# Dealing the inversion's row steps to the slots by their size

## The chip, the cores and the metric

The kernel runs on one core of one Trainium2 chip. The metric is the device time of one execution in microseconds. The times of the kernel before are 2229.79, 2228.49 and 2227.1 us, so the median is 2228.49 us. One further execution was profiled; it took 2232.75 us, of which 2230.4 us lie between its first and its last instruction. The engines are called PE (TensorE), DVE (VectorE), ACT (ScalarE), POOL (GpSimd) and SP (the engine that issues most DMAs).

## What is computed

The reference is a chain of three parts. A delta-rule attention goes through 768 tokens, a soft mixture of eight experts follows, and an MLP closes it:

```
for t in range(768):                     # attention, state 48x48 per head
    y[t] = q[t] @ state
    state = state + b[t] * outer(k[t], v[t] - k[t] @ state)
P = exp(x @ w_gate - max)                # 3072 tokens, 8 experts
for _ in range(8):                       # Sinkhorn
    P /= P.sum(1) + 1e-9;  P /= P.sum(0) + 1e-9;  P *= 3072 / 8
x2 = sum over e of P[:, e] * (relu(x @ w1[e]) @ w2[e])
h = x2 @ w_in;  out = (h * sigmoid(1.702 * h)) @ w_out
```

## The kernel before

The attention is worked in 24 units `u` of 64 tokens for two batches at once, six groups `g` of four units. For a group, the triangular systems inside its units must be inverted first. This is `prep(g)` (line 209), a generator. It computes Gram blocks on PE (tile `pg`, line 182) into `am`, transposes them on DVE into `ln` (line 269), and then inverts 32x32 blocks by rows in a loop over `jj` from 1 to 30. Each `jj` has two DVE instructions: a product into `lt` (line 279) and an addition into `ln` (line 283), both over (31-jj)*jj elements in each of 128 partitions. So they are small at both ends of the loop, 30 elements, and largest in its middle, 240. After the loop DVE transposes the result to `ta` (line 314) and `tt` (line 340), and PE joins the 32x32 blocks to 64x64 (`pz`, line 323, and `px`, line 332). In this text "loop g" is the loop over `jj` of group g; loops 1 to 5 run while the units of the group before are worked.

A unit itself is `chain(u)` (line 357), a serial recurrence in four steps: PE multiplies keys with the state `S` (`ks`, line 373) and DVE makes `r` of it (line 375); PE solves with the inverse (`up`, line 384); PE forms the update (`sp`, line 395) and DVE the new `S` (line 401); PE forms the output (`y`, line 408). One unit later PE transposes the output (`xt`, line 421), ACT and DVE split it into a high and a low part (`xb`, by `split`, lines 495 and 496).

Beside this PE has the first expert as filler: `expert0` (line 642) is cut into 480 items of three matmuls each (`ph` or `po`, lines 499 to 501). ACT and DVE take the `ph` results on (`h`, lines 653 and 654).

The order in which the instructions are written is the order in each engine's queue. It is dealt out by `slot(t)` (line 743), called after each of the 96 steps of the chain. It draws pieces from `prep` until the sum of what they yielded reaches the slot's number in `PIECES` (`FIRST` for the first 16 slots); an item of `prep` yields 1.0, and each half of a `jj` yields 0.5. Between the pieces it calls `expert`, which writes as many items as are due; the share that is due before a piece is weighted with the size of the piece before it. What is left of the 480 items is written after the attention, five at a time between the steps of the Sinkhorn iteration (`psk`, line 711). Then the other experts and the MLP follow, to the end.

Of the kernel before, what the change touches and what calls it, by code (L numbers as in the profile page):

```python
# [40 lines left out]
class Attention:  # L41
# [167 lines left out]
    def prep(self, g):  # L209
# [65 lines left out]
        for jj in range(1, 31):  # L275
            tmp = self.one.tile([128, 256], F32, tag="lt", name="lt")
            nr = 31 - jj
            t3 = tmp[:, 0:nr * jj].rearrange("p (a c) -> p a c", c=jj)
            nc.vector.tensor_tensor(  # L279
                out=t3, in0=ln[:, jj + 1:32, jj:jj + 1].to_broadcast([128, nr, jj]),  # L280
                in1=ln[:, jj:jj + 1, 0:jj].to_broadcast([128, nr, jj]), op=ALU.mult)
            yield 0.5
            nc.vector.tensor_tensor(out=ln[:, jj + 1:32, 0:jj], in0=ln[:, jj + 1:32, 0:jj], in1=t3, op=ALU.add)  # L283
            if (g, jj) in self.at:
                self.at[g, jj]()
            if 0 < g < NG - 1:
                if jj == 17:
                    self.square(w + 2)
                elif jj == 21:
                    self.norm(w + 2)  # L290

            if jj == 22 and 0 < g < NG - 1:
                step = self.weights(w + 2)
            elif jj > 22 and 0 < g < NG - 1:
                next(step, None)
            if jj == 30 and 1 < g < NG - 1:
                self.mask(u + 4)
                self.mask(u + 5)
            yield 0.5
        if g < 2:  # L300
            nc.gpsimd.tensor_copy(out=self.gate, in_=ln[:, 31, 29:30])
            if g == 0:
# [158 lines left out]
def kernel(  # L461
# [257 lines left out]
    def expert_item():  # L719
        while ex:  # L720
            if next(ex[0], None) is not None:
                return True
            ex.pop(0)
        return False
# [5 lines left out]
    while A.ready < 0:  # L730
        next(prep)
# [4 lines left out]
    def expert(n):  # L736

        nonlocal done, due
        due += n
        while done < due and expert_item():  # L740
            done += 1

    def slot(t):

        n, k = rate * ITEMS[t % 16] if t >= LAG else 0, (PIECES if t > 15 else FIRST)[t % 16]
        if t == LAG:
            expert(BURST)
        i = 0
        while i < k:
            expert(n / (k + 1) * step[0])  # L750
            step[0] = next(prep, 1.0)
            i += step[0]
        expert(n / (k + 1))

    step = [1.0]
    build = sums(0, 0)
    for u in range(NU):
        for s, _ in enumerate(A.chain(u)):
            if s == 1 and u > 0:
                if 4 * u >= LAG:  # L760
                    due -= 1
                    expert(1)
                    done += expert_item()
                while u % 2 == 1 and len(ex) > 1:
                    done += expert_item()
                emit_x(u - 1, A.xt())
                if u % 2 == 0:
                    ex.append(expert0(u // 2 - 1))
            if s > 1 and u > 0 and u % 2 == 0:
                (logits if s == 2 else turn)(u // 2 - 1)  # L770
            slot(4 * u + s)
            while A.ready < u // 4:
                next(prep)
            if u > 12:
                next(build, None)
        if u % 2 == 1 and u // 2 + 4 < 12:
            A.load_k(u // 2 + 4)
            A.load_x(u // 2 + 4)
# [415 lines left out]
```

## Time and profile before

| stretch of the profiled execution | us | PE busy | DVE busy | granted PE clock |
|---|---|---|---|---|
| start, first inversion | 0 to 45 | 24.13 | 32.51 | 0.89 |
| first units | 45 to 77 | 23.15 | 23.81 | 0.50 |
| loop 1 | 77 to 115 | 27.30 | 34.14 | 0.74 |
| between loops 1 and 2 | 115 to 165 | 47.84 | 22.18 | 0.83 |
| loop 2 | 165 to 195 | 28.03 | 28.52 | 1.00 |
| between loops 2 and 3 | 195 to 240 | 45.00 | 22.18 | 0.96 |
| loop 3 | 240 to 270 | 28.32 | 28.59 | 1.00 |
| between loops 3 and 4 | 270 to 314 | 43.97 | 23.64 | 1.00 |
| loop 4 | 314 to 344 | 26.41 | 28.45 | 0.94 |
| between loops 4 and 5 | 344 to 390 | 45.43 | 24.26 | 1.00 |
| loop 5 | 390 to 419 | 26.25 | 27.45 | 1.00 |
| last units | 419 to 499 | 80.00 | 19.41 | 0.96 |
| Sinkhorn | 499 to 540 | 34.01 | 29.48 | 0.83 |
| experts and MLP | 540 to 2230 | 1676.98 | 1182.14 | 1.00 |

The profiled execution took 2232.75 us and its span is 2230.4 us. The clock is a share of full speed: 1.00 is 2.4 GHz, 0.50 is 1.2 GHz, and a value between says how long each held. A busy PE may be a slow one, so both columns are read together. DVE instructions have a few tens of ns between them that do not count as busy, so 28.5 of 30 us is an engine without a pause.

### The profile page before, as it was taken

What the parts mean: (1) busy time and instruction counts of PE and PEld (TensorE: products, weight loads), DVE (VectorE), ACT (ScalarE), POOL (GpSimd) and SP (SyncE); (2) the same over time, 40 slices, a digit from 0 to 9 for tenths busy, and PEclk for the clock granted to TensorE, in tenths of its full rate; (3) what the DMA queues carried; (4) which work ended last, traced back from release to release, by engine and by line L of the source; (5) the groups of instructions that cost most, each with busy time, mean ns of one, the idle gap of its engine ahead of it and who ended that gap; (6) DMA issues with size and microseconds to landing.
All of it is one profiled execution on the core that took longest, in us unless ns stands there. A gap on an engine that the chain in (4) does not pass through costs nothing.

```text
span 2230.4 us, 40903 instructions
## 1 busy us (share of the span) xinstructions
PE 2156.8 (97%) x15663; PEld 1953.7 (88%) x15663; DVE 1526.7 (68%) x2792; ACT 1068.0 (48%) x2126; POOL 1096.8 (49%) x1275
## 2 busy tenths in 40 slices
PE   5799999998999999999999999999999999999999
PEld 4778888896989999999999999999999989889998
DVE  7847775627777777767776777777775556776676
ACT  4334434434444544444445444455544446565554
POOL 4141123224776776666552656556665434662333
PEclk8689999998999999999999999999999999999999
DMA  6223333348335343333448655565554465567231
GB/s 159 51 62 81 105 100 102 90 127 294 136 115 184 124 168 136 115 144 110 159 164 275 185 178 182 170 200 178 188 199 143 136 239 164 172 192 246 92 121 50
DMA packets 229154, 336.74 MB, mean 151 GB/s; under 512 B 15648, under 2 KB 192416, under 8 KB 224800
## 3 DMA queue, kind: packets, MB, share of 16 engines
q1 hardware_dynamic: 228096, 332.86, 46.1%
q8 instruction: 123, 2.02, 0.4%
q10 hardware_dynamic: 864, 1.28, 0.2%
q14 instruction: 71, 0.58, 0.1%
HBM read 204.58 MB, written 129.50 MB: 150 GB/s over the span
## 4 chain that ended last, share of the span: by engine, by line
PE 85%; DVE 9%; DMA 2%; POOL 1%; ACT 1%; issue 1%; SPq 0%; POOLq 0%; ACTq 0%; DVEq 0%
PE po L501 14%; PE po L499 14%; PE po L500 14%; PE c L500 11%; PE c L501 11%; PE c L499 11%; DVE lt L279 3%; DVE ln L283 3%; PE ph L499 1%; PE pg L182 1%; PE ph L500 1%; PE ph L501 1%; PE y L408 1%; PE sp L395 1%; PE px L332 1%
## 5 line engine op out<-in xcount | busy, mean ns | idle before, releaser
L501 PE MATMUL po<-w2c,h 128*128 128x384 f32 x1728 | 586.6, 339 | 1.4 <-DVE h L1007 1.3
L500 PE MATMUL po<-w2c,h 128*128 128x384 f32 x1728 | 587.3, 340 | 0.0
L499 PE MATMUL po<-w2c,h 128*128 128x384 f32 x1728 | 578.5, 335 | 1.1 <-ACT h L1005 1.1
L1062 POOL TENSOR_TENSOR acc<-acc,ye 128x384 f32<-128x384 f32 x252 | 261.6, 1038 | 381.7 <-ACT ye L1061 329.6
L501 PE MATMUL c<-xt,w1c 128*128 128x512 f32 x1080 | 429.1, 397 | 2.0 <-POOL w1c L496 2.0
L499 PE MATMUL c<-xt,w1c 128*128 128x512 f32 x1080 | 424.5, 393 | 4.4 <-DVE f L1039 2.3
L500 PE MATMUL c<-xt,w1c 128*128 128x512 f32 x1080 | 428.0, 396 | 0.0
L1039 DVE TENSOR_TENSOR o<-o,c 128x512 f32<-128x512 f32 x288 | 197.5, 686 | 246.7 <-PE c L501 231.5
L1064 DVE SCALAR_TENSOR_TENSOR acc<-po,P,acc 128x384 f32<-128x384 f32 x420 | 258.2, 615 | 150.6 <-PE po L501 150.3
L499 PEld LDWEIGHTS po<-w2c,h 128*128 128x128 f32 x1728 | 324.9, 188 | 41.0 <-ACT h L1005 1.7
L500 PEld LDWEIGHTS po<-w2c,h 128*128 128x128 f32 x1728 | 323.8, 187 | 40.1
L501 PEld LDWEIGHTS po<-w2c,h 128*128 128x128 f32 x1728 | 325.0, 188 | 4.3 <-DVE h L1007 4.3
L1061 ACT ACTIVATE ye<-po,P 128x384 f32<-128x384 f32 x252 | 146.6, 582 | 372.1 <-PE po L501 359.3
L501 PEld LDWEIGHTS c<-xt,w1c 128*128 128x128 f32 x1080 | 202.3, 187 | 47.0 <-POOL w1c L496 2.8
L996 ACT ACTIVATE h<-f 128x512 fp32r<-128x512 f32 x224 | 133.9, 598 | 192.8 <-DVE f L1039 191.0
L499 PEld LDWEIGHTS c<-xt,w1c 128*128 128x128 f32 x1080 | 203.0, 188 | 18.8 <-DVE f L1039 3.1
L1039 DVE TENSOR_TENSOR f<-o,c 128x512 f32<-128x512 f32 x288 | 199.2, 692 | 20.7 <-PE c L501 3.6
L500 PEld LDWEIGHTS c<-xt,w1c 128*128 128x128 f32 x1080 | 203.0, 188 | 9.8
L1032 ACT COPY o<-c 128x512 f32<-128x512 f32 x288 | 163.6, 590 | 59.7 <-PE c L501 58.2
L496 POOL TENSOR_TENSOR w2c<-w2r,w2c 128x384 fp32r<-128x384 f32 x140 | 149.4, 1067 | 47.7 <-ACT w2c L495 47.4
L1074 POOL TENSOR_TENSOR acc<-acc,ye 128x384 f32<-128x384 f32 x84 | 92.7, 1104 | 156.6 <-ACT ye L1073 154.0
L998 DVE SCALAR_TENSOR_TENSOR h<-f,h 128x512 fp32r<-128x512 f32 x224 | 153.1, 683 | 21.2 <-ACT h L996 21.1
(177 smaller groups left out, 3410.2 us busy)
## 6 DMA issues: line engine op xcount, KB each, us to landing
w1c<-wd SPq DMA_DIRECT2D x210, 384.0 KB, 4.4
wd<-w1c SPq DMA_DIRECT2D x28, 1920.0 KB, 7.0
xs<-bo SPq DMA_DIRECT2D x184, 128.0 KB, 2.2
xt<-xs SPq DMA_DIRECT2D x46, 512.0 KB, 6.6
w2r<-in_w_dram SPq DMA_DIRECT2D x55, 384.0 KB, 6.0
wd<-wo SPq DMA_DIRECT2D x56, 256.0 KB, 2.9
w1r<-in_w_dram SPq DMA_DIRECT2D x28, 384.0 KB, 7.6
x<-in_kq_dram SPq DMA_DIRECT2D x24, 384.0 KB, 6.5
```

The costliest lines, as they stand in the source:

```text
L496: eng.tensor_tensor(out=dst_lo, in0=src, in1=dst_hi.bitcast(F32), op=ALU.subtract)
L499: nc.tensor.matmul(ps, lhs[0], rhs[0], start=start, stop=False, **kw)
L500: nc.tensor.matmul(ps, lhs[0], rhs[1], start=False, stop=False, **kw)
L501: nc.tensor.matmul(ps, lhs[1], rhs[0], start=False, stop=stop, **kw)
L996: nc.scalar.activation(out=h[:, 0], in_=src, func=ACTF.Relu)
L998: nc.vector.scalar_tensor_tensor(out=h[:, 1], in0=src, scalar=0.0, in1=h[:, 0].bitcast(F32), op0=ALU.max, op1=ALU.subtract)
L1032: nc.scalar.copy(out=o, in_=ps)
L1039: nc.vector.tensor_tensor(out=d, in0=o, in1=ps, op=ALU.add if how == "add" else ALU.subtract)
L1061: nc.scalar.mul(ye, ps, P[:, u, e:e + 1])
L1062: nc.gpsimd.tensor_tensor(out=a, in0=a, in1=ye, op=ALU.add)
L1064: nc.vector.scalar_tensor_tensor(out=a, in0=ps, scalar=P[:, u, e:e + 1], in1=a, op0=ALU.mult, op1=ALU.add)
L1074: nc.gpsimd.tensor_tensor(out=a, in0=a, in1=ye, op=ALU.add)
```

## The change

A half of a `jj` no longer yields 0.5, but a size that grows with its elements, from 0.285 (30 elements) to 0.618 (240). The sum over a loop stays 30 (it is 29.98). A slot takes pieces until its number is reached to within 0.1, and what it took too much, or too little, is carried over to the next slot.

```diff
@@ prep(g), loop over jj
+            size = 0.238 + 0.785 * nr * jj / 496
             nc.vector.tensor_tensor(   # lt
...
-            yield 0.5
+            yield size
             nc.vector.tensor_tensor(   # ln
...
-            yield 0.5
+            yield size
@@ slot(t)
-        i = 0
-        while i < k:
+        i = over[0]
+        while i < k - 0.1:
             expert(n / (k + 1) * step[0])
             step[0] = next(prep, 1.0)
             i += step[0]
+        over[0] = i - k
         expert(n / (k + 1))
-    step = [1.0]
+    step, over = [1.0], [0.0]
```

No instruction is added or removed. POOL's queue keeps its order. In DVE's queue the chain's instructions change places with neighbouring `lt` and `ln`. In each of loops 2 to 5, counted in `lt` and `ln` instructions of the loop that stand ahead, the first `S` goes from 8 to 11, the first `r` from 24 to 26, `xb` stays at 32, the second `S` goes from 40 to 39 and the second `r` from 56 to 54. In loop 1 the first `r` goes from 8 to 11, `xb` from 14 to 17, the second `r` from 42 to 40.

DVE's queue in loop 4, around the first `r`, before:

```order
L279 TENSOR_TENSOR lt<-ln 128x228
L283 TENSOR_TENSOR ln<-ln,lt 128x19x12
L375 TENSOR_TENSOR r<-ks,v 128x384
L279 TENSOR_TENSOR lt<-ln 128x234
L283 TENSOR_TENSOR ln<-ln,lt 128x18x13
L654 SCALAR_TENSOR_TENSOR h<-ph,h 128x256
L279 TENSOR_TENSOR lt<-ln 128x238
L283 TENSOR_TENSOR ln<-ln,lt 128x17x14
```

and after (line numbers are one higher):

```order
L280 TENSOR_TENSOR lt<-ln 128x228
L284 TENSOR_TENSOR ln<-ln,lt 128x19x12
L280 TENSOR_TENSOR lt<-ln 128x234
L284 TENSOR_TENSOR ln<-ln,lt 128x18x13
L376 TENSOR_TENSOR r<-ks,v 128x384
L280 TENSOR_TENSOR lt<-ln 128x238
L284 TENSOR_TENSOR ln<-ln,lt 128x17x14
L655 SCALAR_TENSOR_TENSOR h<-ph,h 128x256
```

The pair of 234 elements now stands ahead of `r`, which PE's `up` needs.

PE's queue at the end of loop 3, before (`up` and `xt` are the chain's, `po` and `ph` the filler, `pz` the first use of the new inverse):

```order
L384 MATMUL up<-r,tt 64x48 x16
L499 MATMUL po<-w2s_198,h 128x384
L500 MATMUL po<-w2s_198,h 128x384
L501 MATMUL po<-w2s_198,h 128x384
L421 MATMUL xt<-ident,ys 128x128 x3
L499 MATMUL po<-w2s_198,h 128x384
L500 MATMUL po<-w2s_198,h 128x384
L501 MATMUL po<-w2s_198,h 128x384
L323 MATMUL pz<-ta,am 32x32 x32
```

and after:

```order
L385 MATMUL up<-r,tt 64x48 x16
L500 MATMUL po<-w2s_198,h 128x384
L501 MATMUL po<-w2s_198,h 128x384
L502 MATMUL po<-w2s_198,h 128x384
L422 MATMUL xt<-ident,ys 128x128 x3
L324 MATMUL pz<-ta,am 32x32 x32
L500 MATMUL po<-w2s_198,h 128x384
L501 MATMUL po<-w2s_198,h 128x384
L502 MATMUL po<-w2s_198,h 128x384
```

One item of the filler moves behind `pz`. Counted from the last Gram block to the first `pz`, loops 1 and 3 now hold one item less, loop 4 one more, loops 2 and 5 as many as before. When the Sinkhorn iteration begins, one item less has been written, and its last `psk` now stands behind the last item of the filler and ahead of the next stage's first product, where before it stood behind that product.

## Rows read from the trace of the kernel before

**Rows 1.** The page's head: span and instructions.
```profile
span 2230.4 us, 40903 instructions
```

**Rows 2.** Windows, loop 2 and last stage: start:end, length, busy of PE, PEld, DVE, ACT, POOL; clock.
```profile
165.00:195.00 30.00, 28.03 (x412) 25.36 (x412) 28.52 (x85) 10.56 (x26) 4.13 (x4) 1.00 0.39 107
540.00:2230.00 1690.00, 1676.98 (x8478) 1523.92 (x8476) 1182.14 (x1914) 854.99 (x1678) 951.75 (x1102) 1.00 0.49 163
```

**Rows 3.** Waits of PE, 115 to 505 us: total, times, longest.
```profile
PE pz L323 <- DVE ta L314: 4.8, 5, 1.8
PE up L384 <- DVE r L375: 4.5, 3, 2.3
```

**Rows 4.** PE's first `up` in loops 1 to 5: start, us, instruction, wait ahead of it.
```profile
84.77 1.94 PE L384 MATMUL up<-r,tt 64*64 64x48 f32 x32 [6.76 <-DVE r L375]
175.81 1.14 PE L384 MATMUL up<-r,tt 64*64 64x48 f32 x32
251.33 1.14 PE L384 MATMUL up<-r,tt 64*64 64x48 f32 x32 [0.71 <-DVE r L375]
324.15 1.14 PE L384 MATMUL up<-r,tt 64*64 64x48 f32 x32 [2.31 <-DVE r L375]
400.89 1.13 PE L384 MATMUL up<-r,tt 64*64 64x48 f32 x32 [1.49 <-DVE r L375]
```

**Rows 5.** Loop instructions by form, 60 to 505 us: us in total, mean ns of one.
```profile
L283 DVE TENSOR_TENSOR ln<-ln,lt 128x234 f32<-128x234 f32 x10 | 4.0, 402 | 0.3
L279 DVE TENSOR_TENSOR lt<-ln 128x234 f32<-128x234 f32 x10 | 4.0, 399 | 0.2
L279 DVE TENSOR_TENSOR lt<-ln 128x150 f32<-128x150 f32 x10 | 3.5, 348 | 0.2
L283 DVE TENSOR_TENSOR ln<-ln,lt 128x130 f32<-128x130 f32 x10 | 3.0, 295 | 0.3
L279 DVE TENSOR_TENSOR lt<-ln 128x130 f32<-128x130 f32 x10 | 2.9, 290 | 0.0
```

**Rows 6.** First `xb` in loops 2 to 5, in order of time: ACT's half, DVE's half.
```profile
178.23 0.48 ACT L495 CAST xb<-xt 128x384 fp32r<-128x384 f32 x1
178.89 0.55 DVE L496 TENSOR_TENSOR xb<-xt,xb 128x384 fp32r<-128x384 f32 x1
...
253.55 0.48 ACT L495 CAST xb<-xt 128x384 fp32r<-128x384 f32 x1
254.71 0.55 DVE L496 TENSOR_TENSOR xb<-xt,xb 128x384 fp32r<-128x384 f32 x1
...
326.67 0.48 ACT L495 CAST xb<-xt 128x384 fp32r<-128x384 f32 x1 [0.38 <-PE xt L421]
327.53 0.55 DVE L496 TENSOR_TENSOR xb<-xt,xb 128x384 fp32r<-128x384 f32 x1
...
403.11 0.48 ACT L495 CAST xb<-xt 128x384 fp32r<-128x384 f32 x1
404.40 0.55 DVE L496 TENSOR_TENSOR xb<-xt,xb 128x384 fp32r<-128x384 f32 x1
```

**Rows 7.** PE in the Sinkhorn stage: five items of filler, then `psk` with its wait.
```profile
528.61 0.36 PE L499 MATMUL ph<-xb,w1s 128*128 128x256 f32 x1
...
531.71 0.39 PE L711 MATMUL psk<-c,ones 128*128 128x8 f32 x2 [0.74 <-DVE c L708]
```

**Rows 8.** PE's first `pz` behind loops 2 and 5, with the wait.
```profile
194.51 0.66 PE L323 MATMUL pz<-ta,am 32*32 32x32 f32 x31 [0.87 <-DVE ta L314]
...
418.91 1.20 PE L323 MATMUL pz<-ta,am 32*32 32x32 f32 x64 [1.25 <-DVE ta L314]
```

**Rows 9.** Windows behind such waits, columns as in rows 2.
```profile
196.00:200.00 4.00, 4.00 (x73) 3.39 (x72) 0.99 (x1) 1.38 (x3) 0.00 (x0) 0.60 0.21 55
326.00:330.00 4.00, 4.00 (x31) 3.75 (x31) 3.79 (x11) 1.54 (x4) 0.00 (x0) 0.64 0.05 14
401.00:406.00 5.00, 5.00 (x85) 4.56 (x85) 4.69 (x13) 1.91 (x4) 0.00 (x0) 1.00 0.01 3
420.00:428.00 8.00, 8.00 (x120) 7.21 (x114) 2.11 (x2) 2.66 (x6) 2.00 (x3) 0.57 0.22 59
```

## The prediction, as put on record before the result

> **What bounds the kernel now.** I read the stretches first (the table by stage, and [rows 2]). From 540 us to the end PE is busy 1676.98 of 1690 us at clock 1.00, and the change reaches nothing there: three quarters of the span [rows 1] are fixed. The attention ahead of it has two kinds of stretch. Between the loops PE has no pause and DVE is half idle. Inside a loop it is the other way round: from 165 to 195 us DVE is busy 28.52 of 30 us, which with the small pauses between its instructions is an engine that never waits, while PE idles for 2 us. The reader should keep this: a loop lasts as long as DVE needs for all that stands in its queue up to `ta`, and PE's idle time inside it is that length minus the PE work which the program put there.
>
> Next the waits of PE [rows 3]: from 115 us on, 4.5 us for `r` and 4.8 us for `ta`, both made by DVE. So two places matter, the first `r` of a loop and its end. At the first `r` [rows 4] PE waited 6.76 us in loop 1, nothing that the profile counts in loop 2 and 0.71, 2.31 and 1.49 us in loops 3 to 5. DVE has these `r` in its queue behind `lt` and `ln`, so there DVE's order decides and not its speed.
>
> **The change part by part.** *The instructions* are the same ones, and dealing costs nothing on the chip; POOL's queue keeps its order. What has a price is the order on DVE and on PE.
>
> *DVE, the first `r` of loops 2 to 5.* Two more loop instructions stand ahead of it, the pair of 234 elements at 399 and 402 ns [rows 5]: 0.80 us. It comes 0.80 us later in each loop, and so does `up`, since in three of the four loops PE is already waiting there. The reason is in the sizes: the early pieces of the loop are small, and dealt by size a slot takes more of them, so that the first half of the loop moves up in the queue.
>
> *What that does to the loop's length.* DVE's work up to `ta` does not change, so a late `r` alone moves PE's idle time inside the loop from its end to its middle, and costs nothing. It costs where DVE itself runs into a wait. That is `xb`: it stays behind 32 loop instructions, so DVE comes to it at the same time as before, but it needs ACT's half, which follows `up` and `xt` and is 0.80 us later. From [rows 6]: in loop 2 ACT ends at 178.23 + 0.48 = 178.71, with 0.80 at 179.51, and DVE started `xb` at 178.89: 0.62 us of stall. Loop 3: 254.03 + 0.80 = 254.83 against 254.71: 0.12. Loop 4: 327.15 + 0.80 = 327.95 against 327.53: 0.42. Loop 5: 403.59 + 0.80 = 404.39 against 404.40: none. Sum 1.16 us. The bounds: nothing, if the second half of the loops, where `r` and `S` now come earlier, gives it back; and 4 times 0.80 = 3.2 us if each delay comes through whole. I take 1.16, which is nearest to the rows.
>
> *PE, the number of items inside a loop.* Loops 1 and 3 hold one item of the filler less ahead of `pz`, loop 4 one more. An item that leaves a DVE-bound loop has to be done later, where PE has no idle time. Its price: five items ran from 528.61 to the start of the wait before `psk`, 531.71 - 0.74 = 530.97 [rows 7], 2.36 us, so 0.47 us each. Net one item: +0.47 us. Bounds: 0, if the items find idle time elsewhere, and 2 x 0.47 = 0.94 if loop 4 can't use its extra one.
>
> *Loop 1.* `r` comes three instructions later, 0.29 + 0.30 + 0.35 = 0.93 us [rows 5], behind a wait that lasts 6.76 us already. The filler starts behind that `xb`, so PE begins 0.93 us later; but the loop ends when DVE ends it, and DVE does the same work, so beyond the item already counted I charge nothing. Its upper bound is 0.93.
>
> *Sinkhorn.* Its steps wait for DVE, and one item more now lies between them, worth at most 0.47 us of gain. The last `psk` in return loses the product that lay ahead of it. I take 0. SP's order changes only in where two stores of the first expert stand, which nothing waits for.
>
> *Sum.* 1.16 + 0.47 + 0 = +1.6 us. The profiled execution, 2232.75 us, would become 2234.4. It stands 4.26 us above the median, so against the median I forecast 2228.49 + 1.6 = 2230.1 us. By bounds: 2228.5 at the lower end (less 0.5 for Sinkhorn, 2228.0) and 2228.5 + 3.2 + 0.94 + 0.93 = 2233.6 at the upper.
>
> **The clock** is the cost that this sum leaves out. [Rows 9] show that some waits of PE are followed by a stretch near 1.2 GHz: behind the wait of 2.31 us in loop 4 the granted clock was 0.64 from 326 to 330 us, which costs 0.36 x 4 = 1.4 us; behind the wait of 1.25 us before `pz` [rows 8] it was 0.57 for 8 us, 3.4 us; behind the 0.87 us in loop 2 it was 0.60 for 4 us, 1.6 us. Behind the 1.49 us in loop 5 it stayed at 1.00. So the length of a wait alone doesn't tell whether the clock falls. What PE does around it is different as well, for `pz` is 32x32 work.
>
> The Trainium skill, "TensorE: Matmul & The Clock Gate", section "HAM oscillation — how this bites in real kernels", says that waits between bursts of matmuls throw the array back to its lower rate, and that the next burst then starts cold. By that rule every longer wait would be paid twice, which speaks against this change, since it makes the waits at `r` longer; the trace agrees in loop 4 and disagrees in loop 5.
>
> **Rivals.**
>
> *Slower: the longer waits at `r` lower the clock.* By the 0.80 us above, the waits become about 0.8, 1.5, 3.1 and 2.3 us in loops 2 to 5. The last two would reach or pass the 2.31 us that was followed by 0.64. Price: in loops 3 and 5 a new stretch at the lower clock, 1.4 to 3.4 us each, of which loop 5 can hide the 0.45 us that are left of its 1.25 us before `pz`; in loop 4 a second 1.4 us. From 1.4 + 1.0 + 1.4 = 3.8 up to 3.4 + 3.0 + 1.4 = 7.8 us on top of the 1.6, so 2233.9 to 2237.9; I take 2236. It decides once two of the three loops fall. Against it: a slow PE inside a loop eats idle time that it would have had at the loop's end.
>
> *Faster: the wait before `pz` shrinks, and the clock holds there.* Because PE's idle time moves to `r`, the wait before `pz` goes to 1.25 - 0.80 = 0.45 us in loop 5 and 0.87 + 0.62 - 0.80 = 0.69 in loop 2. If the clock then stays up, 3.4 + 1.6 = 5.0 us come back: 2230.1 - 5.0 = 2225.1 us. For it: the stretch of 0.57 is the dearest of all. Against it: 0.69 is hardly less than 0.87.
>
> *Faster: the dealing keeps DVE and PE in step.* Equal DVE time in each slot could remove the waits of [rows 3] altogether, 4.5 + 4.8 = 9.3 us, and the 5.0 us of clock behind `pz`: 2228.5 - 14.3 = 2214 us. Against it: `r` is late in the middle of the loop because the pieces ahead of it are too many already, and the change puts more there; and the loop's length is DVE's work.
>
> *It does not do what it says.* The chain's instructions move by one to three places only, 0.3 to 0.9 us. Then the time stays at 2228.5 within a microsecond, inside the forecast's own range.
>
> **How the numbers follow.** A measurement of this kernel tells about 0.2% from no change, that is 4.5 us: below 2224.0 is faster, above 2232.9 slower. The forecast, with the case of no effect, 48%, own range 2227 to 2233.6; the slower rival 26%, centred on 2236; the wait before `pz` 18%, centred on 2225; keeping step 8%. Faster by over 0.2%: the 8% whole and 12% from the spread around 2225 and unforeseen turns of the clock, 0.20. Slower: the 26% whole and 4% from the upper end of the forecast, 0.30. The rest, 0.50, is within. The range that leaves out no more than 2 in 10 runs from 2222 to 2238 us.
>
> **What would show it.** Right: in loops 2 to 5 the first `up` starts 0.8 us later, counted from the loop's start, behind a longer wait for `r`; the waits before `pz` in loops 2 and 5 are shorter; DVE shows a new wait for ACT's `xb` in loops 2 and 4; the loops last 0 to 0.6 us longer; from the Sinkhorn stage on all is as before, shifted. Wrong: if the waits for `r` shrink, the premise that DVE's queue alone sets them fails. If the sum of the granted clock between 115 and 430 us moves by more than 3 us, the clock decides and not the order, in whichever direction; and if the stage behind 540 us changes by more than a microsecond, I have missed a link there.

## The result and the profile after

The changed kernel took 2240.56 us (median of 4 runs, 2236.36 to 2240.94) against 2227.8 us (4 runs, 2223.58 to 2229.79) of the kernel before beside it: ratio 1.0053, 95% interval [1.0034, 1.0073]. It is slower, and outside the predicted range. Timed once more (run again below) it took 2240.72 against 2222.87 us, ratio 1.0075 [1.0053, 1.0097]. The profiled execution of after is the fastest of its four, 2236.36 us, and that of before, 2232.75 us, is slower than any of before's four; so the pair of profiles differs by 4.0 us of span only, where the medians differ by 12.8.

The page's head and the last stage, to compare with [rows 1, 2] (columns as there):

```profile
span 2234.4 us, 40904 instructions
```
```profile
540.00:2234.00 1694.00, 1682.48 (x8503) 1528.06 (x8501) 1186.84 (x1923) 857.56 (x1683) 957.09 (x1109) 1.00 0.49 164
```

The last stage runs at clock 1.00 as before. So I followed the attention, by the first up of each loop (to compare with [rows 4]: start, us, instruction, wait ahead of it):

```profile
85.54 1.94 PE L385 MATMUL up<-r,tt 64*64 64x48 f32 x32 [7.74 <-DVE r L376]
...
177.01 1.14 PE L385 MATMUL up<-r,tt 64*64 64x48 f32 x32 [1.45 <-DVE r L376]
...
252.58 1.53 PE L385 MATMUL up<-r,tt 64*64 64x48 f32 x32 [1.69 <-DVE r L376]
...
327.54 1.42 PE L385 MATMUL up<-r,tt 64*64 64x48 f32 x32 [3.11 <-DVE r L376]
...
410.09 1.94 PE L385 MATMUL up<-r,tt 64*64 64x48 f32 x32 [2.78 <-DVE r L376]
```

In loops 2 to 5 the waits are 1.45, 1.69, 3.11 and 2.78 us where 0.8, 1.5, 3.1 and 2.3 were forecast. That step was nearly right. But `up` itself takes 1.53, 1.42 and 1.94 us in loops 3 to 5; in [rows 4] it took 1.14 in every loop after the first. The first `pz` behind the loops (to compare with [rows 8]) and the waits of PE from 115 to 505 us (with [rows 3]):

```profile
196.23 1.20 PE L324 MATMUL pz<-ta,am 32*32 32x32 f32 x64 [1.48 <-DVE ta L315]
...
271.90 1.20 PE L324 MATMUL pz<-ta,am 32*32 32x32 f32 x64 [1.09 <-DVE ta L315]
...
347.33 1.20 PE L324 MATMUL pz<-ta,am 32*32 32x32 f32 x64 [1.05 <-DVE ta L315]
...
429.79 1.38 PE L324 MATMUL pz<-ta,am 32*32 32x32 f32 x64 [1.51 <-DVE ta L315]
```
```profile
PE up L385 <- DVE r L376: 9.0, 4, 3.1
...
PE pz L324 <- DVE ta L315: 5.1, 4, 1.5
```

The waits for `r` doubled, from 4.5 to 9.0 us, and those before `pz` did not shrink as the faster rival had it: behind loops 2 and 5 they grew from 0.87 and 1.25 to 1.48 and 1.51. The windows behind these waits (to compare with [rows 9]):

```profile
252.00:260.00 8.00, 7.42 (x88) 6.81 (x89) 6.27 (x17) 2.87 (x6) 0.00 (x0) 0.79 0.15 46
...
327.00:335.00 8.00, 7.46 (x91) 6.86 (x92) 6.73 (x18) 2.19 (x5) 0.00 (x0) 0.79 0.21 65
349.00:357.00 8.00, 8.00 (x112) 7.18 (x111) 1.50 (x3) 4.35 (x7) 0.36 (x1) 0.50 0.61 173
410.00:418.00 8.00, 7.91 (x96) 7.43 (x97) 6.36 (x16) 2.65 (x6) 0.00 (x0) 0.79 0.20 61
```

Before, only loop 4 had such a stretch at its first `up`. After, loops 3, 4 and 5 have one, and one more, at 1.2 GHz from 349 to 357 us, lies behind the `pz` of loop 4. What the stretch does to DVE is seen in loop 3 (ACT's and DVE's half of `xb`, to compare with [rows 6]):

```profile
256.04 0.48 ACT L496 CAST xb<-xt 128x384 fp32r<-128x384 f32 x1 [0.92 <-PE xt L422]
```
```profile
256.56 0.56 DVE L497 TENSOR_TENSOR xb<-xt,xb 128x384 fp32r<-128x384 f32 x1 [1.39 <-ACT xb L496]
```

PE's slow work delays `xt`, ACT waits 0.92 us for it, and DVE, which sets the loop's length, stands still for 1.39 us. In loop 5 DVE waits 1.01, 0.25 and 0.37 us in the same way, for `h` and `xb`. Over loops 2 to 5 DVE's own waits rise from 0.22 to 6.04 us; part of that is not the clock's, for loop 2, at clock 1.00, has 1.08 us of it, and loop 4 waits 0.70 us for `h` at its start, ahead of `up`.

Counted from the first `lt` to the end of `ta`, loops 2 to 5 took 29.65, 29.42, 32.13 and 30.04 us before and 31.17, 31.22, 33.65 and 32.92 after: 121.2 and 129.0 in sum, +7.7. The gaps between a loop and the next are 4.6 us longer behind loop 4 (49.55 against 44.94) and 1.5 shorter behind loop 2, where before's profile had its own stretch. After is 10.9 us late at the end of loop 5, 9.5 at the first `psk`, 5.4 at the last and 4.0 at the end. Most of what comes back lies in the Sinkhorn stage, where before's profile ran at clock 0.83 from 499 to 540 us and after's at 1.00: that is a difference of these two executions, and no experiment was about it.

### The profile page after: what moved, and what is told of

It is laid out like the page before. It is cut to its first block, busy times and chain, and to the rows that moved or that the text cites. A ratio compares the mean times of both kernels' runs of the same rounds, so it can differ in the third digit from the quotient of the medians.

```text
span 2234.4 us, 40904 instructions
## 1 busy us (share of the span) xinstructions
PE 2156.7 (97%) x15663; PEld 1952.2 (87%) x15663; DVE 1526.5 (68%) x2792; ACT 1068.5 (48%) x2126; POOL 1097.5 (49%) x1275
## 4 chain that ended last, share of the span: by engine, by line
PE 86%; DVE 9%; ACT 2%; DMA 1%; issue 1%; POOL 1%; SPq 0%; POOLq 0%; ACTq 0%; DVEq 0%
PE po L502 14%; PE po L500 14%; PE po L501 14%; PE c L501 11%; PE c L502 11%; PE c L500 11%; DVE ln L284 2%; DVE lt L280 2%; PE pg L182 1%; PE ph L500 1%; PE ph L501 1%; PE ph L502 1%; PE up L385 1%; PE y L409 1%; PE sp L396 1%
```

## The experiments

Theory K (the clock): the late first `r` and the early second `r` make PE wait longer, the granted clock falls behind these waits, and PE's slow work comes back to DVE, so that the loops grow. Rival O: the new order on DVE costs by itself. Every kernel was timed beside the kernel before on the same chip; the table collects what each profile, one execution each, shows. The wait is that ahead of the first `up`, the clock that of the 8 us from its start, taken to the whole us; a wait that PE spent at other instructions instead counts as 0. In busy and busypz the wait is what the spare matmuls left of it. The sum is that of loops 2 to 5, each from the first `lt` to the end of `ta`.

```
kernel    ratio to before            loop 3: wait clock us    loop 5: wait clock us    sum
before    1                                0.71  1.00 29.42         1.49  1.00 30.04  121.2
rlate     1.0013 [0.9999, 1.0027]          1.57  1.00 29.62         2.36  1.00 30.71  123.6
srlate    1.0016 [1.0003, 1.0029]          1.70  1.00 29.67         2.72  1.00 30.62  123.0
rearly    1.0021 [1.0009, 1.0034]          0     1.00 29.40         0.63  1.00 30.61  124.0
mirror    1.0024 [1.0012, 1.0036]          0.28  1.00 31.01         0.43  1.00 30.40  126.8
headback  1.0019 [1.0006, 1.0032]          0.72  1.00 30.27         1.76  0.79 31.45  124.7
tail      1.0031 [1.0019, 1.0043]          0.98  1.00 29.84         1.89  0.79 32.25  126.2
tailback  1.0034 [1.0022, 1.0046]          1.31  1.00 29.81         2.79  0.59 32.95  126.4
items     1.0062 [1.0043, 1.0080]          1.96  1.00 29.96         2.69  0.65 33.51  126.6
norm1     1.0063 [1.0042, 1.0084]          1.55  1.00 29.91         2.19  0.60 34.13  126.9
after     1.0053 [1.0034, 1.0073]          1.69  0.79 31.22         2.78  0.79 32.92  129.0
again     1.0075 [1.0053, 1.0097]          1.55  0.79 31.05         2.78  0.64 34.63  130.2
warm      1.0054 [1.0038, 1.0069]          0     1.00 32.12         0     1.00 29.94  129.1
busy      1.0020 [1.0006, 1.0035]          0.30  1.00 29.65         0.69  1.00 31.51  124.8
busypz    0.9996 [0.9983, 1.0008]          0.19  1.00 29.56         0.69  1.00 31.32  124.7
```

**The first r late, alone (rlate), and early (rearly).**

```diff
-PIECES = (4, 2, 2, 1, 2, 4, 4, 4, 4, 4, 4, 4, 3, 3, 2, 2)
+PIECES = (4, 2, 2, 1, 2, 4, 4, 5, 3, 4, 4, 4, 3, 3, 2, 2)   # rlate: first r at 26, not 24
+PIECES = (4, 2, 2, 1, 2, 4, 4, 3, 5, 4, 4, 4, 3, 3, 2, 2)   # rearly: first r at 22
```

> The kernel before (all pieces of 0.5), with one row step of loops 2 to 5 moved from the slot behind the first r to the slot ahead of it (PIECES 5, 3 in place of 4, 4), so that r stands behind 26 loop instructions and not 24, and S, xb and the second r stay where they were. Theory A (a late first r is what costs: PE waits longer at it, ACT's half of xb and the h behind it come later, and DVE, which works in order, then stands still for them): waits at the first up of about 0.8, 1.5, 3.1 and 2.3 us in loops 2 to 5, DVE waits for xb of 0.3 to 1.4 us, the loops 0.8 to 2 us longer each, 3 to 9 us in all, the kernel 0.2 to 0.4% slower than before. Rival B (the weighting of the filler and the places of S and h cost): within 2 us of before. Rival C (only the granted clock moves, by chance): loops as long as before, any time between -5 and +10 us.

> The kernel before with one row step of loops 2 to 5 moved the other way (PIECES 3, 5): the first r stands behind 22 loop instructions and not 24, all else as before. Theory A: the waits at the first up shrink by 0.8 us, to none in loops 2 and 3, about 1.5 in loop 4 and 0.7 in loop 5; DVE had hardly a wait in these loops before (27.3 to 30.0 us from the first lt to ta), so the loops can't get much shorter: 0 to 3 us faster. Rival B: within 1 us of before. Rival C: loops as long as before, the time wherever the clock takes it.

The late `r` makes the waits of after, 1.57, 3.18 and 2.36 us in loops 3 to 5, and DVE's stall for `xb` is 0.45 + 0 + 0.68 + 0 = 1.13 us: the 1.16 of my sum. But the clock holds in loops 3 and 5, with `up` at its 1.14 us, and little time is lost (0.13%, with an interval that reaches to none):

```profile
252.47 1.14 PE L384 MATMUL up<-r,tt 64*64 64x48 f32 x32 [1.57 <-DVE r L375]
...
402.97 1.13 PE L384 MATMUL up<-r,tt 64*64 64x48 f32 x32 [2.36 <-DVE r L375]
```

So the late `r` is not the whole cost, and a long wait at `up` is not always followed by a fall. An earlier `r` is no gain either: PE then waits at the filler's `ph` instead, 1.4 us in loop 3 and 3.25 in loop 4.

**The sizes turned round (mirror), and the filler as before (items).**

```diff
+            size = 0.762 - 0.785 * nr * jj / 496                    # mirror
...
+        goal = due + n                                              # items, in slot
+            expert(min(n / (k + 1) * step[0], goal - due))
+        expert(goal - due)
```

> The changed kernel with the sizes turned round: 0.762 - 0.785 * nr * jj / 496, so that small pieces count for much and large ones for little; the sum over a loop stays 30. In loops 2 to 5 the first S stands behind 6 loop instructions (before 8, changed 11), the first r behind 22 (24, 26), xb behind 33 (32, 32), the second S behind 43 (40, 39), the second r behind 57 (56, 54). Theory A: the waits at the first up as short as with the early r, the loops no longer than before, the time 0 to 4 us under that of before; what could spoil it is the second r, now later by one. Rival B: as the weighting differs from before as much as in the changed kernel, some 5 to 12 us slower than before. Rival C: no prediction but for equal loops.

> The changed kernel, but each slot brings the filler to just the sum that it had before the change, so that the number of items of the filler ahead of each step of the chain is that of before; the order of lt, ln, S, r and xb on DVE stays that of the changed kernel. Theory A: the cost is in DVE's order, so the time stays within 4 us of the changed kernel, 8 to 13 us above before, loops of 29 to 31.5 us. Rival B: the items moved out of loops 1 and 3, and h at other places, were the cost: within 3 us of before.

In mirror the first `r` stands earlier than before's, which was to make it faster (theory A); it is 0.24% slower. Its loops grow to 126.8 us, in which DVE waits 4.5 us for `h` and `r`, though the clock is 1.00 at the first `up` of loops 3 to 5. So an order can cost without a fall there; mirror's clock fell elsewhere (0.72 from 338 to 350 us).

In items each slot brings as many filler items as before; the loss is that of the changed kernel. So the weighting of the filler, my term of +0.47, is not where the time goes.

**Loop 1 as before (norm1); first S and first r both late (srlate).**

```diff
+            size = 0.238 + 0.785 * nr * jj / 496 if g > 1 else 0.5   # norm1
-PIECES = (4, 2, 2, 1, 2, 4, 4, 4, 4, 4, 4, 4, 3, 3, 2, 2)
+PIECES = (4, 2, 2, 1, 2, 5, 4, 4, 3, 4, 4, 4, 3, 3, 2, 2)            # srlate
```

> The changed kernel with 0.5 for the pieces of loops 0 and 1, so that loop 1 is as before and loops 2 to 5 as changed (S 11, r 25 or 26, xb 32, second r 54). Theory K and rival O: the cost is made in loops 2 to 5, waits at the first up 1.5, 1.7, 3.1 and 2.8 us, ratio 1.004 to 1.006. Rival L (what the change does in loop 1, where the first r stands at 11 instead of 8 and TensorE waits 7.7 instead of 6.8 us, makes it): ratio 1.000 to 1.002.

> The kernel before with two numbers of PIECES moved (5, 4, 4, 3 in places 5 to 8): first S at 10 and first r at 26 updates in loops 2 to 5 (before 8 and 24), all else at 32, 40, 56 as before; loop 1 as before. Theory K, with the waits at the first up as the only link: like the run with r late alone, waits 0.6, 1.6, 3.2 and 2.4 us, loops 115 us in sum, ratio 1.000 to 1.003, unless the clock falls in loops 3 or 5 too, which then shows there as ups of 1.5 to 1.9 us. Rival O, that S and r late together make the cost: VectorE waits 3 us for xb and 2.9 for h at full clock, loops 120 us in sum, ratio 1.004 to 1.006.

norm1 has the whole loss, so loop 1 has no part in it. srlate is like rlate: the early half of the loops alone gives 0.16%, interval 0.03 to 0.29%.

**The late half (tail, tailback, headback).** In loops 2 to 5 the change also puts the second `S` at 39 instead of 40 and the second `r` at 54 instead of 56.

```diff
+PIECES = (4, 2, 2, 1, 2, 4, 4, 4, 4, 4, 4, 3, 4, 3, 2, 2)   # tail: before, second r at 54
+PIECES = (4, 2, 2, 1, 2, 4, 4, 4, 4, 5, 4, 4, 2, 3, 2, 2)   # tailback: after, second r at 57
+PIECES = (4, 2, 2, 1, 2, 3, 4, 4, 5, 4, 4, 4, 3, 3, 2, 2)   # headback: after, first r at 24
```

> The kernel before with the second r of loops 2 to 5 at 54 updates instead of 56 (PIECES 3, 4 in places 11 and 12), all else as before. Theory T (the late half of the loops costs: with the second r earlier, two updates more stand between it and ta, TensorE is done with its chain earlier and waits longer for ta at the first pz, and the clock falls behind it): waits at pz behind loops 2 to 5 near 1.5, 1.0, 1.0 and 1.5 us instead of 0.9, 0.3, 0.6 and 1.3, half clock behind one or two of them, ratio 1.003 to 1.006. Rival H (the early half, S and first r, with all three at once): ratio 1.000 +-0.001.

> The changed kernel with the late half put back: PIECES 5 in place 9 and 2 in place 12, so that in loops 2 to 5 the second S stands at 40 and the second r at 57 (changed: 39 and 54; before: 40 and 56); first S 11, first r 26, xb 32 and loop 1 as changed. Theory T: the waits at pz shrink to 0.1 to 1.0 us, ratio 1.001 to 1.003, that of the early half alone (S and r late: 1.0016). Rival H: ratio stays at 1.004 to 1.006.

> The changed kernel with the early half put back: PIECES 3 in place 5 and 5 in place 8, so that in loops 2 to 5 the first S stands at 9 and the first r at 24 (changed: 11 and 26; before: 8 and 24); xb 32, second S 39, second r 54 and loop 1 as changed. Theory T: the waits at the first up go back to 0.7, 2.3 and 1.5 us in loops 3 to 5, those at pz stay at 1.0 to 1.5, and the ratio stays at 1.003 to 1.005. Rival H: ratio 1.000 to 1.002.

Neither theory named there was right about the halves. The late half alone costs 0.31%, putting it back leaves 0.34%, putting the early half back leaves 0.19%: each half is a part, and within the intervals they add up. The waits before `pz` behind loops 2 to 5 did fall in tailback, to 0.70, 0.22, 0.55 and 0.57 us, and stayed long in headback, at 1.43, 0.90, 1.40 and 1.50. So in the changed kernel it is the early second `r` that makes them long: PE is through with its chain sooner, `ta` comes no sooner. In before's order it does not make all of them long: tail has 0.39, 0.56, 0.75 and 2.15 us.

**The changed kernel again.**

> The changed kernel once more, for its time beside the others of this call and for a second profiled execution. Ratio 1.004 to 1.007. If the half-clock stretches come from the order, they stand where the first profile had them: at the first up of loops 3, 4 and 5 and behind pz of loop 4 (350 to 357 us). Rival (they come by chance from one execution to the next): at other places, with waits of the same length.

```profile
255.16 1.14 PE L385 MATMUL up<-r,tt 64*64 64x48 f32 x32 [1.55 <-DVE r L376]
...
333.02 1.14 PE L385 MATMUL up<-r,tt 64*64 64x48 f32 x32 [3.10 <-DVE r L376]
...
410.86 1.95 PE L385 MATMUL up<-r,tt 64*64 64x48 f32 x32 [2.78 <-DVE r L376]
```
```profile
255.00:263.00 8.00, 7.84 (x91) 7.17 (x92) 6.73 (x18) 2.87 (x6) 0.00 (x0) 0.79 0.27 85
333.00:341.00 8.00, 7.98 (x94) 7.32 (x95) 7.28 (x20) 2.39 (x6) 0.00 (x0) 0.79 0.39 123
411.00:419.00 8.00, 8.00 (x89) 7.55 (x90) 6.29 (x16) 2.29 (x5) 0.00 (x0) 0.64 0.23 71
```

The waits are those of the first profile to 0.15 us, and the same three loops have the slow stretch. Behind `pz` the place changes: the gaps are longer behind loops 2 and 3 (47.34 and 44.70 against 44.46 and 41.77 us) and not behind loop 4 (45.17).

**The filler moved into the waits (warm, warmb).**

```diff
-ITEMS = (6, 5, 5, 5, 5, 5, 5, 5, 5, 5, 5, 6, 5, 5, 5, 5)
+ITEMS = (6, 5, 5, 5, 5, 5, 5, 8, 8, 2, 2, 6, 5, 5, 5, 5)   # warm, in the changed kernel
+ITEMS = (6, 5, 5, 5, 5, 5, 5, 7, 7, 3, 3, 6, 5, 5, 5, 5)   # warmb, in the kernel before
```

> The changed kernel with its filler moved: ITEMS 8, 8, 2, 2 instead of 5, 5, 5, 5 in places 7 to 10, so that TensorE has 6 to 7 items (before 4 to 5) between ks and the first up of loops 2 to 5; the order of the inverses on VectorE stays as changed (S 11, r 26, xb 32, second r 54). Theory K (the long waits at the first up let the clock fall, up is stretched from 1.14 to 1.5-1.9 us, and xb and h on VectorE then wait): the waits of 1.45, 1.69, 3.11 and 2.78 us fall to under 1 us (under 1.5 in loop 4), the clock at the first up of loops 3 and 5 is 1.00, VectorE waits under 1.5 us for xb in sum instead of 3.1, loops 2 to 5 take 28.3, 27.5, 30.8 and 28.6 us (sum 115 +-1 instead of 120.5), and the time is 1 to 5 us above before, ratio 1.0005 to 1.0025. Rival O (the order of S, r, xb and second r on VectorE costs by itself): loops 2 to 5 stay at 29.1, 29.1, 31.5 and 30.8, ratio 1.004 to 1.006.

> The kernel before with ITEMS 7, 7, 3, 3 in places 7 to 10: 6 to 7 items between ks and the first up of loops 2 to 5, VectorE's order as before. Theory K: the waits of 0.71, 2.31 and 1.49 us go, the half-clock stretch at the first up of loop 4 (0.59) goes, and 2 to 5 us are won: ratio 0.998 to 0.999. Rival O: VectorE sets the loops alone (no wait of its own in loops 2 to 5 of before but 0.22 us), so filler moved ahead of up saves nothing: ratio 1.000 +-0.001; should y then come late for xb, 1 to 2 us are lost.

Both theories missed. The waits at `up` went, but PE then waited for DVE's `h`, and warmb lost as well: 1.0063 [1.0042, 1.0084]. In warm, loop 4:

```profile
321.54 0.58 PE L500 MATMUL ph<-xb,w1s 128*128 128x256 f32 x1 [2.73 <-DVE h L655]
...
342.94 0.39 PE L500 MATMUL ph<-xb,w1s 128*128 128x256 f32 x1 [2.10 <-DVE h L655]
```

Filler has a chain of its own through DVE, so this pair does not part K from O.

**The waits filled with spare matmuls (busy, busypz).** These leave the order of all other instructions as it was; PE works where it would idle. The products go into the tile that the true matmul then overwrites.

```diff
         up = self.psc.tile([128, H, D], F32, tag="c", name="up")
+        for h in range(H * {6: 1, 10: 1, 14: 2, 18: 2}.get(u, 0)):        # busy and busypz
+            for b in range(2):
+                nc.tensor.matmul(up[tk[b], h % H], tt[tk[b], 8 * uu + h % H], self.V[w][tk[b], j, h % H],
+                                 start=True, stop=True)
...
             ps = self.psg.tile([128, n, 32], F32, tag="g", name="pz")
+            for m in range(n if m0 == 0 and g in (2, 3, 4, 5) else 0):     # busypz
+                for q in (0, 64):
+                    nc.tensor.matmul(ps[q + 32:q + 64, m], am[q:q + 32, m, 32:64], am[q:q + 32, m, 0:32],
+                                     start=True, stop=True, tile_position=(q, q + 32))
```

> The changed kernel with spare matmuls right ahead of the first up of loops 2 to 5 (tt times v into up's own tile, which up then overwrites): 16, 16, 32 and 32 of them, of up's shape, 1.14 us a pass of 16 at full clock. The order on all engines and the chain stay as changed. Theory K (the fall of the clock is what costs): the waits of 1.45, 1.69, 3.11 and 2.78 us become 0.3, 0.5, 0.8 and 0.5, the clock at the first up of loops 3, 4 and 5 is 1.00, up takes 1.14 us, loops 2 to 5 take 30.3, 29.8, 32.6 and 30.8 us instead of 31.2, 31.2, 33.5 and 33.8 (first lt to end of ta), and 4 to 8 us come back: ratio 1.002 to 1.004, the rest being the clock behind pz and the later r. Rival O (the order on VectorE costs): clock 1.00, but loops and time as changed, ratio 1.005 to 1.007.

> As busy, and 32 spare matmuls of pz's shape ahead of the first pz of loops 2 to 5 (a part of the matrix that is there already, into pz's own tile). Theory K: besides what busy gives, no half-clock stretch between the end of a loop and the next, gaps 44.5, 42.0 and 44.9 us; ratio 1.000 to 1.002. Rival O: 1.005 to 1.007.

Here the theories part, and K's ratios are met (busypz's even passed a little), O's are not. In busypz the first `up` of loops 2 to 5, the clock in loops 3 and 5, and the clock from 115 to 430 us:

```profile
172.44 1.14 PE L393 MATMUL up<-r,tt 64*64 64x48 f32 x32 [0.34 <-DVE r L380]
...
247.50 1.14 PE L393 MATMUL up<-r,tt 64*64 64x48 f32 x32 [0.19 <-DVE r L380]
...
321.06 1.13 PE L393 MATMUL up<-r,tt 64*64 64x48 f32 x32 [1.02 <-DVE r L380]
...
398.25 1.14 PE L393 MATMUL up<-r,tt 64*64 64x48 f32 x32 [0.69 <-DVE r L380]
```
```profile
247.00:255.00 8.00, 7.81 (x113) 7.06 (x110) 7.53 (x20) 3.23 (x7) 0.00 (x0) 1.00 0.33 104
...
398.00:406.00 8.00, 7.75 (x104) 7.27 (x105) 7.51 (x20) 2.82 (x7) 0.00 (x0) 1.00 0.35 109
115.00:430.00 315.00, 308.67 (x5276) 272.57 (x5277) 207.95 (x533) 133.23 (x275) 83.46 (x93) 0.98 0.34 91
```

With the same order on DVE, and a first `up` that starts 12.07, 11.60, 13.92 and 13.25 us behind the start of loops 2 to 5 where after's starts at 12.10, 12.04, 14.01 and 13.36, the clock is 1.00 at each first `up`, `up` takes 1.14 us, loops 3 and 5 take 29.56 and 31.32 us instead of 31.22 and 32.92, and the gaps behind loops 2 to 4 are 44.37, 41.68 and 45.24. Filling `up` takes the loss from 0.53-0.75% to 0.20%, filling `pz` too takes it to nothing, 2224.59 against 2224.05 us, though PE has 448 more matmul instructions by the page's count (16111 against 15663).

That does not make the order free. busypz also fills the waits behind which the kernel before has stretches of its own: from 115 to 430 us its clock is 0.98, before's 0.95. Its 12 runs took 2224.5 us in the mean at a mean clock of 0.9816, where the kernel before took 2222.0 at 0.981 (24 runs) and 2221.4 at 0.982 (17 runs). So about 3 us, an estimate from these means, are left to the order and the spare matmuls; rlate and srlate, with the clock held in loops 3 and 5, lost as much (0.13 and 0.16%). The clock is the larger part of the 12.8 to 17.9 us, not all of it.

**The same in the kernel before, and loop 1 filled.** busyb has spare matmuls at the first `up` of loops 4 and 5 and at `pz` behind loops 2 and 5; busyb4 fewer at `up` and all of `pz`; busyall is busyb with loop 1's waits, busy1 is busypz with loop 1's waits.

```diff
+        for h in range(H * {14: 2, 18: 1}.get(u, 0)):                  # busyb; pz at g in (2, 5)
+        for h in range(H * {14: 1, 18: 1}.get(u, 0)):                  # busyb4; pz at g in (2, 3, 4, 5)
+        for h in range(H * {2: 3, 14: 2, 18: 1}.get(u, 0)):            # busyall; pz at g in (1, 2, 5)
+        for h in range(H * {2: 4, 6: 1, 10: 1, 14: 2, 18: 2}.get(u, 0)):   # busy1; pz three times at g = 1
```

> The kernel before with 32 and 16 spare matmuls ahead of the first up of loops 4 and 5 (waits of 2.31 and 1.49 us) and 32 ahead of the first pz behind loops 2 and 5 (0.87 and 1.25). Theory K: loop 4 without its half-clock stretch, 1 to 2 us shorter, no stretch behind loops 2 and 5, 2 to 4 us won, ratio 0.998 to 0.999. Rival O: no change, ratio 0.9995 to 1.0005, or slower by what the spare matmuls take, 1.0005 to 1.001.

> As busyb, and in loop 1 48 spare matmuls ahead of the first up (a wait of 6.76 us at half clock) and 32 ahead of the first pz behind it (1.83). Theory K: the clock is back at 1.00 some 5 us earlier in loop 1 and stays there behind it; TensorE waits for VectorE there, so the loop itself gets 0 to 2 us shorter and the stretch behind it 1 to 3; ratio 0.997 to 0.999. Rival O: as busyb.

> The kernel before with 16 spare matmuls ahead of the first up of loops 4 and 5 and 32 ahead of the first pz of loops 2 to 5. Theory K: half-clock stretches at up of loop 4 and behind pz of loops 2 and 5 go, 2 to 4 us won, ratio 0.998 to 0.999, if no gap of 1.4 us without issue appears. Rival (the spare matmuls cost by themselves, as filling the kernel before has cost so far): ratio 1.001 to 1.003, and the profile shows such a gap again or a wait of over 2 us at ph.

> As busypz (the changed kernel with spare matmuls at the first up and the first pz of loops 2 to 5), and in loop 1 64 spare matmuls ahead of the first up (a wait of 7.7 us, at half clock) and 96 ahead of the first pz behind it (a wait of 4.5 us, followed by clock 0.50 to 0.80). Theory K: the stretch behind loop 1 goes, the gap between loops 1 and 2 shrinks from 47.6-51.1 to about 44 us, ratio 0.997 to 0.999. Rival (the clock behind loop 1 comes back at the same time whatever stands in the wait): ratio as busypz, 0.9990 to 1.0005.

K's gain did not come: 1.0025 [1.0010, 1.0039], 1.0013 [1.0000, 1.0025], 1.0035 [1.0015, 1.0055] and 1.0013 [1.0000, 1.0027]. busy1 held its clock from loop 2 on as busypz did, but its gap behind loop 1 stayed at 47.94 us. It is no test of that place: ahead of the last of its spare matmuls for `pz` PE paused for 2.14 us, so the wait was not filled. In the kernel before the stretch at the first `up` of loop 4 did go, but busyb's profile has a new one, behind a pause in which PE waited for nothing that the profile shows, the line and then its window:

```profile
211.85 0.92 PE L182 MATMUL pg<-x 48*64 48x128 f32 x13 [1.43 <-issue]
```
```profile
212.00:226.00 14.00, 14.00 (x112) 11.20 (x110) 7.73 (x22) 1.55 (x4) 1.94 (x2) 0.57 0.01 2
```

Its gap behind loop 2 is 52.88 us instead of 45.92. busyall has such a pause of 1.42 us at 283.9, busyb4 two, of 1.15 and 1.08 us, with clocks of 0.51, 0.55 and 0.63 over the 14 us behind them; before, after and busypz have none over 0.3 us between 45 and 540 us.

The traces tell what PE waited for: its own next instructions. Number PE's records in a trace from the start, matmuls, weight loads and those of its sequencer: these four pauses and busy1's of 2.14 us end at 5825 (busyb and busyb4), 8385, 10689 and 3265, each 193 above a multiple of 256. The page's queue "q8 instruction" moved 123 packets of 16 KB in before for 31588 such records, one for about 256, and such a packet began 2.4 to 3.2 us before each of the five pauses ended. The kernel before has such pauses in its first 45 us, the longest of 1.59 us at 25.2, and there too each over 0.4 us ends 193 above a multiple of 256. Why the packet came late just there is not shown, nor whether every execution has the pause. So no version here beats the kernel before, and what before would take with its own stretches gone is not known.

## Why the prediction was wrong

- *The first r of loops 2 to 5, 0.80 us later.* Right in the main: the waits came out within 0.65 us of the forecast ones. Counted from the loop's start, `up` came 1.0, 1.0, 1.5 and 1.2 us later; 0.70 of loop 4's is DVE's wait for `h`, which the sum did not have.
- *DVE's stall for xb, 1.16 us.* The sum was met by the late `r` alone (1.13 in rlate), by some luck: 0.45, 0, 0.68 and 0 us by loop, where 0.62, 0.12, 0.42 and 0 were forecast. In after DVE stalls for 6.04 us, 3.13 for `xb` and 2.9 for `h`; in busypz, with the same order and the clock held, 2.0 us of it are left, so about 4 us come from PE's slow work between `up` and `xt`. Of the order's own share only a part was in the sum: busypz's loops 2 to 5 are 3.4 us longer than before's, not 1.2, and before's loop 4 holds a slow stretch of its own.
- *The step that failed: "The clock is the cost that this sum leaves out."* I had the rows, named the mechanism and gave it 26% at 2236 us, but forecast the sum without it, so a term that became the largest stood at nothing. busy and busypz show its size: with the waits filled the changed kernel goes from 0.53-0.75% over before to 0.20% and then to none, and the order keeps about 3 us of the 12.8 to 17.9. The rival's price was about right per stretch (1.4 to 3.4 us forecast; loop 3 lost 1.4 to 1.6 us and loop 5 2.2 to 4.0 us against rlate and srlate), and its condition, two of the three loops falling, was met; it missed the stretches behind `pz`, and even its upper end, 2237.9 us, lies under the 2240.56 measured.
- *What spoke against that rival:* that a slow PE eats idle time it would have had at the loop's end. Wrong: `xt`, and through it DVE's `xb`, hang on PE right behind `up`, so the stretch lies on DVE's path.
- *"The wait before `pz` shrinks."* Wrong. I moved PE's idle time from the loop's end to `r` and forgot that the second `r`, two places earlier, takes PE through the rest of its chain sooner. I had counted that as a possible gain. It holds for the changed kernel (headback against tailback), not in general (tail).
- *Loop 1, items, Sinkhorn.* No part of the loss (norm1, items); Sinkhorn's 3 to 4 us between the two profiles are the clock again, with nothing to show that the order made them.
- *The marks that I set.* The clock from 115 to 430 us was 0.95 in before's profile and 0.94 and 0.93 in after's two, where 0.01 of 315 us is 3.2 us: a move of 3 to 6 us, to the side that the result took. It pointed to the clock; busy and busypz decided. The other mark, over a microsecond in the last stage, tells nothing: from the last `psk` to the end before took 1694.8 us, after 1693.4 and again 1694.6, and the other profiles lie between 1690.3 and 1700.1.

The Trainium skill, "TensorE: Matmul & The Clock Gate", section "HAM oscillation — how this bites in real kernels", has a kernel in which the matmuls behind each wait for data start cold. After's loops 3 to 5 agree, at waits of 1.69, 3.11 and 2.78 us; rlate's and srlate's loop 5 do not, at 2.36 and 2.72 us.

What stays open is what decides, beside the wait itself, whether the clock falls. tail, which has before's order of `S` and `r` up to that place, fell behind 1.89 us in loop 5; srlate held behind 2.72.

## What to carry to other kernels

A wait of TensorE can have two prices, its length and the clock behind it, and here, where a chain leads from the slow matmuls back to the engine that sets the pace, the second was the larger: put it into the sum, not beside it. To learn whether the clock or the order costs, fill the wait with spare matmuls into a tile that is overwritten anyway. It leaves the other engines' order as it is, but it fills waits that the kernel before has as well, and it moves PE's instruction count, so look for new pauses and compare at the same mean clock. Moving useful filler into the wait is no such test, since filler has waits of its own.

## What the runs showed of the hardware

The time of one and the same kernel goes with the mean clock granted to the run: of the kernel before, 17 runs at 0.977 took 2229.1 us in the mean and 24 runs at 0.981 took 2222.0. The clock fell behind waits as short as these: behind 1.05 us before `pz` after's clock was 0.50 from 349 to 357 us, and behind busyb's pause of 1.43 us it was 0.57 for 14 us. It held behind waits as long as 2.72 us (srlate, loop 5). PE's queue can run dry at steps of 256 of its instructions, for 1.1 to 2.1 us in four of the kernels with spare matmuls. And each execution has its own falls, so a stretch behind `pz` in one profile tells little of the median, while those at `up` came back in both profiles of the changed kernel.
